# Issuing every second regrouping copy of a talking-heads attention from GpSimd

## The chip, the cores and the metric

One core of one Trainium2 chip runs the whole program. The metric is the device time of one execution in microseconds (us). The kernel before took 912.95, 916.15 and 916.83 us in three runs, so its median is 916.15 us.

## What is computed

Three layers follow each other on 1792 tokens (4 batches of 448): an attention whose 12 heads are mixed before and after the softmax ("talking heads"), a feed-forward layer, and a soft mixture of experts.

```python
scores = scale * np.matmul(q, k.transpose(0, 1, 3, 2))
scores = np.einsum('bhij,hg->bgij', scores, w_pre)
scores = scores - np.max(scores, axis=-1, keepdims=True)
attn = np.exp(scores)
attn = attn / (np.sum(attn, axis=-1, keepdims=True) + 1e-09)
attn = np.einsum('bhij,hg->bgij', attn, w_post)
attn_out = np.matmul(attn, v)
...
h = x @ w_in
x = (h - np.tanh(h)) @ w_out
...
logits = x @ phi        # softmaxes over tokens and over slots, 8 experts of 4 slots each
```

All tensors are float32. The change lies in the first layer alone.

## The kernel before

**Chunks and steps.** Each batch's 448 rows are cut into chunks of 120, 120, 120 and 88 rows, 16 chunks in all. TensorE makes the scores of a chunk head by head (`scores`), and ScalarE copies them into the tile `S`, which has the chunk's rows on partitions and heads by keys along them. The mix over heads needs the heads on partitions. So a chunk is taken in 12 (for the short chunk 10) steps of up to 10 rows, and for each step one DMA, the regrouping copy (`regroup`, line 312), moves the 10 rows with their 12 heads from `S` into 120 partitions of a tile `D`: 120 pieces of 1792 bytes, 210 KB. There are 184 steps.

**The order in a step.** The loop at line 566 writes out the order of the work by hand. In every step `s` it first issues the regrouping copy of step `s + 4` (`D_AHEAD`), then the loads and stores planned for this step. Steps are worked off in pairs. In an even step TensorE runs `premix(s)` on the two tiles `D` of steps `s` and `s + 1` (line 321), VectorE takes the maxima (325), TensorE runs `postmix` of the pair four steps back (364), ScalarE the exponentials (333), and GpSimd adds a small number to their sums (`guard`, 339). In the odd step VectorE takes the reciprocal (343), GpSimd multiplies the mixing weights by it (`norm`, two instructions of line 350), and ScalarE gathers the result of `postmix` (378). Scores of the next chunk, value products (403) and conversions of the feed-forward weights (lines 48 to 69) are spread over the steps. Of each of the 64 conversion pieces GpSimd does one addition (line 69).

**Buffers and queues.** There are six tiles `D`, used in turn. So the copy of step `s + 4` needs the tile of step `s - 2`, and has to wait until `premix(s - 2)` has read it. The copy of the odd step after it needs the tile of step `s - 1`, which the same `premix` reads. All DMAs of this stage are issued by SyncE (SP), one after another in the order of the program: the regrouping copies, the loads of `q`, `k`, `v` and raw weights (`f`), and the stores of converted weights (`wi`, `wo`) and of attention results (`xd`). GpSimd issues none.

The names in the diff: `D_AHEAD` is 4, `NH` is 12, `ds` is the list of the six tiles `D`, `chunks[n][2]` the rows of chunk `n`, and `rows(s)` gives a step's chunk, first row and number of rows.

Of the kernel before, what the change touches and what calls it, by code (L numbers as in the profile page):

```python
# [16 lines left out]
NB, NH, SEQ, HD = 4, 12, 448, 64  # L17
# [113 lines left out]
def talking_heads(tc, ident, q, k, v, w_pre, w_post, xd, box, follow):  # L131
    nc = tc.nc
# [4 lines left out]
    D_AHEAD = 4  # L137
# [17 lines left out]
    S_t, D_t = {}, {}  # L155
# [147 lines left out]
    def rows(s):  # L303
        n, kk = slots[s]
        o, m = chunks[n][3][kk]
        return n, o, m

    def regroup(s):
        n, o, m = rows(s)
        t = ds[s % DB]  # L310
        ni, w = chunks[n][2], len(chunks[n][3])
        nc.sync.dma_start(out=t[4:4 + m * NH], in_=S_t[n][o:ni:w])
        D_t[s] = t

    def premix(s):
# [133 lines left out]
    for m in range(1, NC):  # L449
        w = len(chunks[m - 1][3])  # L450
# [11 lines left out]
    for m in range(1, NC):  # L462
        if chunks[m][1] + CHUNK >= SEQ and m + 1 < NC:
            w = len(chunks[m - 1][3])
            w0 = start[m - 1] - D_AHEAD
            free_at = {}
            for p in range(NP):
                t = w0 + HEAD_LAG + p // 2 * w // 3 + 1 + p % 2
# [16 lines left out]
    t = 2  # L485
    for i, j in enumerate(pieces):
# [10 lines left out]
        t = h  # L497
# [18 lines left out]
    for hi, lo, cost, f, a in sorted(wanted, key=lambda z: (z[0] - z[1], z[0])):  # L516
        s = min(range(lo, hi + 1), key=crowd)
# [36 lines left out]
    for s in range(D_AHEAD):  # L554
        regroup(s)
# [9 lines left out]
    s = 0  # L565
    while s < NS + T_LAG + 3 or jobs or late:
# [3 lines left out]
        if s + D_AHEAD < NS:  # L570
            regroup(s + D_AHEAD)
# [898 lines left out]
```

## Time and profile before

| what | value |
|---|---|
| median of three runs | 916.15 us (912.95 to 916.83) |
| the profiled execution | 922.78 us, its span 921.1 us |
| TensorE matmul busy | 841.1 us (91% of the span) |
| ScalarE, VectorE busy | 574.2 us (62%), 559.1 us (61%) |
| GpSimd busy | 250.6 us (27%) |
| DMA | 224.53 MB, mean 244 GB/s |

The span is the time from the first to the last instruction of the profiled execution. Busy times leave out instructions that only wait or issue a DMA. In rows of the trace, PE is TensorE's matmuls, PEld its weight loads, DVE is VectorE, ACT ScalarE, POOL GpSimd and SPq the queue of SyncE. `out<-in` names tiles, L312 is line 312. The attention with its steps takes the first 465 us or so of the span.

### The profile page before, as it was taken

What the parts mean: (1) busy time and instruction counts of PE and PEld (TensorE: products, weight loads), DVE (VectorE), ACT (ScalarE), POOL (GpSimd) and SP (SyncE); (2) the same over time, 40 slices, a digit from 0 to 9 for tenths busy, and PEclk for the clock granted to TensorE, in tenths of its full rate; (3) what the DMA queues carried; (4) which work ended last, traced back from release to release, by engine and by line L of the source; (5) the groups of instructions that cost most, each with busy time, mean ns of one, the idle gap of its engine ahead of it and who ended that gap; (6) DMA issues with size and microseconds to landing.
All of it is one profiled execution on the core that took longest, in us unless ns stands there. A gap on an engine that the chain in (4) does not pass through costs nothing.

```text
span 921.1 us, 28684 instructions
## 1 busy us (share of the span) xinstructions
PE 841.1 (91%) x11750; PEld 599.0 (65%) x11750; DVE 559.1 (61%) x1183; ACT 574.2 (62%) x1351; POOL 250.6 (27%) x431
## 2 busy tenths in 40 slices
PE   7868998979998798999979999999999998999995
PEld 6536666656666566766668777667776776875553
DVE  2445776757777577788545567566766677740103
ACT  2756786857877687888756576546664666730013
POOL 3134343534444344455412223000000014610000
PEclk7988998999999999999989999999999999998998
DMA  4699797997988978787467968669764536879998
GB/s 109 180 194 217 232 232 215 231 224 217 234 235 229 228 220 223 220 248 239 152 226 234 320 236 306 222 252 353 304 216 161 171 110 217 301 308 425 424 374 311
DMA packets 147286, 224.53 MB, mean 244 GB/s; under 512 B 61268, under 2 KB 128852, under 8 KB 143572
## 3 DMA queue, kind: packets, MB, share of 16 engines
q1 hardware_dynamic: 143808, 209.84, 73.4%
q10 hardware_dynamic: 3348, 12.87, 3.7%
q8 instruction: 93, 1.52, 0.7%
q14 instruction: 37, 0.30, 0.1%
HBM read 147.96 MB, written 36.18 MB: 200 GB/s over the span
## 4 chain that ended last, share of the span: by engine, by line
PE 64%; DMA 12%; ACT 9%; DVE 8%; issue 4%; POOL 1%; SPq 1%; ACTq 0%; POOLq 0%; DVEq 0%
PE hp L813 24%; DMA D<-S 8%; PE pm L321 6%; PE vx L403 5%; PE tm L364 5%; PE sc L287 4%; ACT e L333 4%; DVE mx L325 3%; PE h L1255 3%; PE gt L884 3%; PE so L1296 2%; PE tz L1275 2%; ACT S L295 2%; DMA rg<-wi 2%; PE lgp L934 2%
## 5 line engine op out<-in xcount | busy, mean ns | idle before, releaser
L333 ACT ACTIVATE e<-pm,mx 128x448 f32<-128x448 f32 x184 | 115.2, 632 | 94.6 <-DVE mx L325 92.4
L364 PEld LDWEIGHTS tm<-wk,e 64*64 64x64 f32 x5888 | 120.3, 139 | 65.8 <-issue 40.5
L325 DVE TENSOR_REDUCE mx<-pm 128x1 f32<-128x448 f32 x184 | 105.9, 616 | 83.8 <-PE pm L321 83.8
L813 PE MATMUL hp<-xa,rg 128*128 128x512 f32 x576 | 152.4, 404 | 0.0
L364 PE MATMUL tm<-wk,e 64*64 64x60 f32 x5888 | 128.7, 225 | 18.8 <-issue 9.5
L321 PE MATMUL pm<-D,wpre 64*64 64x448 f32 (+2 forms) x736 | 116.3, 579 | 25.0 <-DMA D<-S 19.6
L813 PEld LDWEIGHTS hp<-xa,rg 128*128 128x128 f32 x576 | 102.4, 188 | 28.5 <-issue 10.5
L295 ACT ACTIVATE S<-sc 120x448 f32<-120x448 f32 (+1 forms) x186 | 91.4, 552 | 12.6 <-PE sc L287 6.3
L350 POOL TENSOR_SCALAR wk<-wpost,rv 128x60 f32<-128x60 f32 x184 | 89.6, 510 | 16.0 <-DVE rv L343 13.5
L339 POOL TENSOR_SCALAR rv<-ss 128x2 f32<-128x2 f32 x92 | 26.2, 285 | 248.5 <-ACT e L333 214.8
L287 PE MATMUL sc<-khi,qT 64*120 64x448 f32 (+1 forms) x384 | 85.4, 407 | 6.6 <-DVE xs L413 4.4
L403 PE MATMUL vx<-aT,vn 128*64 128x120 f32 (+1 forms) x1536 | 88.1, 269 | 0.8 <-issue 0.8
L775 POOL TENSOR_TENSOR rg<-rg 128x384 fp32r<-128x384 f32 x32 | 32.0, 1013 | 205.5 <-DVE rg L772 191.7
L403 PEld LDWEIGHTS vx<-aT,vn 128*64 128x64 f32 x1536 | 77.8, 141 | 6.9 <-issue 3.4
L844 DVE SCALAR_TENSOR_TENSOR qd<-qd,sq 128x512 f32<-128x512 f32 (+1 forms) x62 | 38.3, 618 | 69.7 <-ACT mk L840 63.2
L833 ACT ACTIVATE sq<-hp 128x512 f32<-128x512 f32 (+1 forms) x62 | 32.8, 530 | 71.8 <-PE hp L813 71.8
L378 ACT ACTIVATE aT<-tm 128x480 f32<-128x480 f32 x144 | 75.9, 593 | 0.1
L813 PE MATMUL hp<-xb,rg 128*128 128x512 f32 x288 | 74.7, 404 | 0.0
L69 POOL TENSOR_TENSOR fa<-fa,f 128x384 f32<-128x384 f32 x64 | 67.3, 1052 | 8.1 <-DVE rv L343 3.6
L321 PEld LDWEIGHTS pm<-D,wpre 64*64 64x64 f32 (+2 forms) x736 | 25.4, 134 | 63.5 <-DMA D<-S 25.1
L813 PEld LDWEIGHTS hp<-xb,rg 128*128 128x128 f32 x288 | 52.0, 188 | 16.6 <-issue 6.3
L287 PEld LDWEIGHTS sc<-khi,qT 64*120 64x120 f32 (+1 forms) x384 | 46.9, 182 | 22.7 <-issue 5.4
(184 smaller groups left out, 1393.5 us busy)
## 6 DMA issues: line engine op xcount, KB each, us to landing
ex<-in_moe_w_dram SPq DMA_DIRECT2D x25, 1536.0 KB
D<-S SPq DMA_DIRECT2D x144, 210.0 KB
rg<-wis SPq DMA_DIRECT2D x32, 768.0 KB
f<-in_moe_w_in_dram SPq DMA_DIRECT2D x32, 384.0 KB
f<-in_moe_w_out_dram SPq DMA_DIRECT2D x32, 384.0 KB
wis<-rg ACTq DMA_DIRECT2D x16, 768.0 KB
rg<-wi SPq DMA_DIRECT2D x26, 384.0 KB
wi<-fa SPq DMA_DIRECT2D x32, 192.0 KB
```

The source lines that it names most:

```text
L69: eng.tensor_tensor(out=out, in0=bits(a), in1=bits(p), op=ALU.add)
L287: nc.tensor.matmul(xs[e][0][:ni], lhsT=qT[n][s, l, p, :ni], rhs=kt[s], start=(i == 0), stop=(i == 2))
L295: nc.scalar.activation(out=dst, in_=xs[e][0][:ni], func=ACTF.Copy)
L321: nc.tensor.matmul(xs[x][64 * i:64 * i + 64], lhsT=wpre[k0:k1], rhs=d[i][k0:k1], start=True, stop=True)
L325: nc.vector.tensor_reduce(out=mx[:, x:x + 1], in_=xs[x], op=ALU.max, axis=AX.X, negate=True)
L333: nc.scalar.activation(out=es[x], in_=xs[x], func=ACTF.Exp, bias=mx[:, x:x + 1], accum_out=ss[:, x:x + 1])
L350: nc.gpsimd.tensor_scalar(out=wk, in0=wpost, scalar1=rv[:, x:x + 1], scalar2=None, op0=ALU.mult)
L364: nc.tensor.matmul(xs[i][64 * z:64 * z + 64, x, c], lhsT=es[x][h, j:j + 64], rhs=wks[x][h], start=True, stop=True)
L378: nc.scalar.activation(out=out[:, :, c0:c0 + m].rearrange("p a (x i) -> p a x i", x=2), in_=x, func=ACTF.Copy)
L403: nc.tensor.matmul(x[64 * e:64 * e + 64, i, :ni], lhsT=nat_v[b, h // NP][:, h % NP, c, :], rhs=a[:, c, h, :ni], start=(c == 0), stop=(c == ...
L813: nc.tensor.matmul(hp, lhsT=r32(w[:, m, hl, cs]), rhs=r32(x_of(b, c, l)), start=(c == 0 and i == 0), stop=(c == KD - 1 and i == 2))
L844: nc.vector.scalar_tensor_tensor(out=qd, in0=qd, scalar=TG_E, in1=sq, op0=ALU.add, op1=ALU.mult)
```

## The change

In `regroup`, the copies of even steps from step 4 on are issued from GpSimd's queue; the first four and all odd ones stay on SyncE's. That is 90 of the 184 copies. What is copied, from where and to where, and the place of the call in the program stay as they are; nothing else is edited.

```diff
@@ -309,7 +309,8 @@
         n, o, m = rows(s)
         t = ds[s % DB]
         ni, w = chunks[n][2], len(chunks[n][3])
-        nc.sync.dma_start(out=t[4:4 + m * NH], in_=S_t[n][o:ni:w])
+        queue = nc.gpsimd if s >= D_AHEAD and s % 2 == 0 else nc.sync
+        queue.dma_start(out=t[4:4 + m * NH], in_=S_t[n][o:ni:w])
         D_t[s] = t
```

## Rows read from the trace of the kernel before

**Rows 1.** The page: the chain that ended last, shares of the span by line.

```profile
PE hp L813 24%; DMA D<-S 8%; PE pm L321 6%; PE vx L403 5%; PE tm L364 5%; PE sc L287 4%; ACT e L333 4%; DVE mx L325 3%; PE h L1255 3%; PE gt L884 3%; PE so L1296 2%; PE tz L1275 2%; ACT S L295 2%; DMA rg<-wi 2%; PE lgp L934 2%
```

**Rows 2.** Stretches: start:end and length, busy us per engine (instructions), clock, DMA share.

```profile
26.00:465.00 439.00, 389.55 (x8502) 276.69 (x8502) 301.21 (x693) 330.19 (x864) 181.79 (x344) 0.96 0.84 221
...
44.00:83.00 39.00, 28.28 (x510) 18.74 (x507) 18.73 (x44) 23.16 (x58) 13.88 (x32) 0.82 0.98 199
...
178.00:205.00 27.00, 21.98 (x435) 15.31 (x431) 15.78 (x36) 16.10 (x41) 10.75 (x19) 0.94 0.94 218
...
270.00:315.00 45.00, 37.33 (x827) 26.20 (x826) 29.92 (x72) 31.49 (x82) 20.25 (x35) 1.00 0.92 234
...
400.00:465.00 65.00, 60.92 (x1580) 44.22 (x1574) 46.08 (x109) 51.61 (x135) 29.87 (x59) 1.00 0.67 206
```

**Rows 3.** Who waited for whom: total us, times, longest; one line's durations, ns.

```profile
PEld pm L321 <- DMA D<-S: 25.1, 19, 3.2
PE pm L321 <- DMA D<-S: 19.6, 20, 4.1
...
L312 SPq DMA_DIRECT2D D<-S x184: 714/816/5522, 26.4 to 460.2; - x184
```

**Rows 4.** The chain in order of time, 25:31 and 44:83: start, us, what.

```profile
26.36 2.84 DMA D<-S
...
44.84 7.56 DMA vn<-in_v_dram
...
52.47 11.67 DMA D<-S
```

**Rows 5.** SyncE's queue in order of time, 178:206: start, us, line, copy.

```profile
179.81 0.81 SPq L312 DMA_DIRECT2D D<-S  x1
...
181.25 0.81 SPq L312 DMA_DIRECT2D D<-S  x1
...
184.86 0.83 SPq L312 DMA_DIRECT2D D<-S  x1
186.11 0.34 SPq L118 DMA_DIRECT2D wo<-fa  x1
188.15 0.57 SPq L390 DMA_DIRECT2D xd<-xs  x1
188.82 2.85 SPq L312 DMA_DIRECT2D D<-S  x2
```

**Rows 6.** TensorE in order of time, 178:206: in brackets idle before, and releaser.

```profile
194.87 0.93 PE L321 MATMUL pm<-D,wpre 64*64 64x448 f32 x2 [0.82 <-DMA D<-S]
198.07 0.60 PE L321 MATMUL pm<-D,wpre 64*64 64x448 f32 x3 [2.27 <-DMA D<-S]
```

**Rows 7.** SyncE's own waits, 26:470: total us, times, longest us.

```profile
SPq L312 <- PE tm L364: 53.1, 63, 3.4
...
SPq L390 <- DMA D<-S: 3.4, 2, 1.8
```

**Rows 8.** GpSimd's groups, 26:465: count, busy us, mean ns, idle before and releasers.

```profile
L350 POOL TENSOR_SCALAR wk<-wpost,rv 128x60 f32<-128x60 f32 x180 | 87.9, 512 | 11.1 <-DVE rv L343 8.6 <-PE sc L287 2.2
...
L69 POOL TENSOR_TENSOR fa<-fa,f 128x384 f32<-128x384 f32 x64 | 67.3, 1052 | 8.1 <-DVE rv L343 3.6 <-DVE f L64 0.4
...
L339 POOL TENSOR_SCALAR rv<-ss 128x2 f32<-128x2 f32 x90 | 25.8, 287 | 244.3 <-ACT e L333 210.6 <-DMA D<-S 15.8 <-DMA f<-in_moe_w_in_dram 5.3
```

**Rows 9.** GpSimd in order of time, 178:206 and 436:441.

```profile
184.49 0.95 POOL L350 TENSOR_SCALAR wk<-wpost,rv 128x60 f32<-128x60 f32 x2
187.97 0.22 POOL L339 TENSOR_SCALAR rv<-ss 128x2 f32<-128x2 f32 x1 [2.53 <-ACT e L333]
...
437.03 1.02 POOL L69 TENSOR_TENSOR fa<-fa,f 128x384 f32<-128x384 f32 x1 [0.37 <-DVE f L64]
439.08 0.22 POOL L339 TENSOR_SCALAR rv<-ss 128x2 f32<-128x2 f32 x1 [1.03 <-ACT e L333]
```

**Rows 10.** TensorE in order of time, 438:444.

```profile
439.36 0.98 PE L321 MATMUL pm<-D,wpre 64*64 64x448 f32 x8
...
443.00 0.98 PE L321 MATMUL pm<-D,wpre 64*64 64x448 f32 x8
```

**Rows 11.** VectorE, one group of the conversions, 26:465: as in rows 8.

```profile
L52 DVE TENSOR_SCALAR fa<-fa 128x384 f32<-128x384 f32 x64 | 29.9, 468 | 0.0
```

## The prediction, written before the changed kernel ran

> **What bounds the kernel now.** I read the chain first. TensorE's work leads it, but the regrouping copy D<-S is its second entry with 8% of the span, about 74 us [rows 1]. A copy stands on the chain from its issue to its landing, so those 74 us are not idle time. What TensorE itself stood still for a copy is in the waits: 19.6 us in 20 waits of matmuls, and 25.1 us in 19 waits of weight loads [rows 3]. Weight loads and matmuls overlap, so the two are the same stalls seen twice and not a sum. 25 us (2.7%) is the most that can be won by copies that land earlier.
>
> Next, where the stalls lie. Over the 439 us of the attention the 16 DMA engines are busy to 0.84 and TensorE for 389.55 us [rows 2]. Three stretches stand out, with DMA shares of 0.98, 0.94 and 0.92, in which TensorE idles for 39.00 - 28.28 = 10.7, 27.00 - 21.98 = 5.0 and 45.00 - 37.33 = 7.7 us, together 23 us [rows 2]. That agrees with the 20 to 25 us above. At the end, from 400 to 465 us, the share is 0.67 and TensorE is 94% busy [rows 2].
>
> Then, why a copy is late. With nothing else under way it lands 2.84 us after its issue; in a loaded stretch one takes 11.67 us [rows 4]. Three things lengthen it. The copy queues behind loads on the same DMA engines. SyncE issues one DMA at a time, 0.816 us for a typical copy [rows 3], and first waits for a free tile: 53.1 us in 63 waits [rows 7]. And SyncE waits for the landing of earlier DMAs that have nothing to do with the next one: on the chain a load of v, issued at 44.84, lands 7.56 us later, and only then, at 52.47, the copy goes out [rows 4]; the store of attention results waits twice for copies D<-S, which it neither reads nor writes [rows 7]. So only so many DMAs of SyncE's queue may be under way at once.
>
> **The pair.** `premix` needs both tiles of a pair, and the odd step's copy is issued last: in one stalled pair 181.25 against 179.81, in the next 188.82 against 184.86, with another store or two between [rows 5]. That is 1.4 and 4.0 us later, though both tiles come free with the same `premix`. For the pair whose even copy went out at 184.86, TensorE waits 0.82 us at the first matmul (even tile) and 2.27 us at the third (odd tile; each product is two matmuls in fp32) [rows 6]. The odd copy decides most of the stall.
>
> **The change part by part.** *Removed from SyncE:* 90 issues of 0.816 us [rows 3], 73 us of its queue in 439 us, and the wait for a free tile that stands before each. What was queued behind an even copy, the loads and stores of that step and then the odd copy, moves up. The odd copy gains at least the 0.8 us of the even issue, and at most the whole lag, 1.4 to 4.0 us in the two pairs. I take 0.8 us for every stalled copy, near the lower end, because the DMA engines are nearly full there and an earlier issue partly only queues longer. There are some 20 waits in the trace, in about 15 pairs (an estimate: pairs with two waits count once), so 15 x 0.8 = 12 us. The upper end is all 25 us. The lower end is 0, if the engines' rate alone sets the time.
>
> *Added to GpSimd:* 90 issues. The trace has no DMA issued there. The nearest rows are the same copy issued by SyncE, 0.71 us at the least and 0.816 at the median [rows 3], GpSimd's own pass over 128 partitions at 1.05 us [rows 8], and as an upper end two such passes, 2.1 us. I take 1.05, an engine's own work on as many rows, so 95 us. In the program the issue stands before `guard`, ahead of which GpSimd idles 244.3 us in 90 times, 2.7 us each [rows 8]; it is waiting for the exponentials there. That covers 1.05 us in nearly all steps; the thinnest of the rows shown is 1.03 us [rows 9]. At 2.1 us many would reach over by some 0.5 us. What is queued behind is `guard`, then the reciprocal on VectorE, `norm`, and the additions of the conversions. `postmix` uses `norm`'s result only four steps later, so TensorE sees little: 0 to 3 us in all, taken as 1. Without the cover 90 x 1.05 = 95 us would stand on GpSimd's path. GpSimd's busy time goes from 181.79 [rows 2] to 277 of 439 us; it doesn't become the bound.
>
> *Waits moved to GpSimd:* the copy's waits for a free tile and for the chunk's last scores. GpSimd comes to the even copy only after the pair's `norm`, which lies well behind the `premix` that frees the tile; and ScalarE writes the scores before the exponentials for which `guard` would wait anyway. Both cost nothing.
>
> *Later start of the even copies:* SyncE runs ahead and issues when the tile is free. GpSimd comes to it after its work of the step before. For the copy that SyncE issued at 184.86 it would be ready at 184.49 + 0.95 = 185.44 with `premix` at 194.87, so 9.4 us ahead [rows 6, 9]. Late in the stage it is ready at 437.03 + 1.02 = 438.05 with `premix` at 443.00, 4.95 us ahead [rows 9, 10]. From the even copy's issue 1.05 us go for issuing and at least 2.84 - 0.82 = 2.0 us to land [rows 3, 4], 3.1 in all; the loaded price is up to 11.67. A queue of its own spares it the waiting behind SyncE's loads, so I take 5 us. Then the late pairs are short by 0.1 us and some more where traffic is dense: 2 us in all, between 0 and the 11 us of the third rival.
>
> What comes out: -12 + 1 + 2 = -9 us. On the profiled execution 922.78 becomes 914; it lies 6.6 us over the median of the runs, so for the median 916.15 - 9 = 907 us. The later layers start when the attention ends and are fed by loads issued then; I carry the gain over whole.
>
> Two rules of the Trainium skill bear on this. "DMA: Bandwidth & Descriptors", section "Issuing engines are not separate DMA queues", says that DMAs run on the same 16 engines whoever issues them, and that a second issuer saves only the sequencer's time. By it alone the sum would be nearer 0 than -9. The same page, section "Queues, rings and completion order", says that a copy is spread over the largest number of engines up to 16 that divides the outer dimensions of both sides, for SyncE's queue the lowest-numbered ones; that would be 10 for 120 and 10 rows, and that GpSimd's copies take all 16 or go round. By it the even copies would leave ten crowded engines, and the gain would be larger. No row here shows single engines.
>
> **The rivals.**
> *Same.* The engines' rate is the limit where the stalls are: DMA shares of 0.92 to 0.98 [rows 2] speak for it. What the even copies gain in their own queue is taken from the odd copies and loads, and 15 x 0.8 falls to 15 x 0.2 = 3 us, eaten up by 1 + 2. Time 916, within 4 us. Against it: SyncE waits for landings and free tiles while those shares are reached [rows 7], and the odd copy's lag of 1.4 to 4.0 us is issue order and no lack of rate [rows 5]. The skill's first rule above is this rival.
>
> *Larger gain.* Odd copies move up by the full lag, even ones by the shorter queue: the 20 to 25 us of stalls go nearly whole, some 900 to 895 us. For it: stalls of 0.82 and 2.27 us [rows 6] are no longer than the lags. Against it: those shares again.
>
> *Slower.* One mechanism: the even copies of GpSimd land too late. If issue and landing take 7 us in place of 5, a pair like that at 443.00 is short by 7 - 4.95 = 2 us. Pairs follow each other in 443.00 - 439.36 = 3.64 us there [rows 10], so 400 to 465 us holds about 18. A late `premix` puts off GpSimd's next copies too, and with six tiles the loop closes over three pairs, so about 18 / 3 x 2 = 12 us are lost, with as much again in the dense stretches, against up to 12 us won. Net 0 to +12; at 8 us, +10 and more. It decides from about 6.5 us on. For it: 11.67 us is seen in a loaded stretch [rows 4], and a GpSimd issue is unpriced. Against it: in the last stretch the DMA share is only 0.67 [rows 2]. Place: `premix` waits at its first matmul, on the even tile. Time 916 to 930.
> The skill's page "SBUF — State Buffer", section "SBUF: two separate sides", feeds this rival: descriptors written by GpSimd are held up while VectorE runs an instruction that takes the port pair they share. Here line 52 could be one, 64 times 0.468 us [rows 11], too little to decide by itself.
>
> That the change doesn't do what it says can be left out: the diff changes the issuing queue and nothing else.
>
> **How the numbers follow.** The forecast, 4.6 us to about 15 us faster, has 0.44; the larger gain 0.10; same 0.27; slower by over 4.6 us 0.19. 0.5% of 916 is 4.6 us, about what a measurement of this kernel can tell from no change. Faster is 0.54, same 0.27, slower 0.19. For the range I leave out a gain over 21 us (0.06) and a loss over 6 us (0.14): 895 to 922 us. The forecast's own range is 901 to 911.5.
>
> **What would show it.** Right: 94 copies of line 312 on SyncE, 90 on GpSimd; the odd copy issued about when the even one was; TensorE's waits for D<-S down from 19.6 to about 8 us; the three stretches shorter; GpSimd's idle before line 339 down by about 95 us with no longer period of pairs. Wrong: an issue on GpSimd well over 2 us; waits at the first matmul of `premix` from 400 us on; the same stalls at the third matmul. A changed clock or a longer MoE stage would be nothing that I foresaw.

## The result: the changed kernel is about 1% slower

| | median | runs from .. to | ratio to before, 95% interval |
|---|---|---|---|
| before | 916.49 us | 912.95 .. 918.65 | |
| changed | 929.46 us | 926.93 .. 929.77 | 1.0109 [1.0075, 1.0142] |

The forecast was 907 us with a range of 895 to 922; the kernel was 13 us slower in place of 9 us faster. The changed kernel was timed again beside a later set of experiments (`after2`): 1.0093 [1.0058, 1.0129]. The profiled execution took 926.93 us, with a span of 925.2 us.

Line numbers behind the edit are higher by one: `premix` is now line 322, the copy 313, `guard` 340. The page of the changed kernel has, in its chain by line, the copies' share unchanged at 8% (as in [rows 1]):

```profile
PE hp L814 24%; DMA D<-S 8%; PE vx L404 6%; PE pm L322 6%; PE tm L365 4%; ACT e L334 4%; PE sc L287 4%; DVE mx L326 3%; DMA ex<-in_moe_w_dram 3%; PE gt L885 3%; PE lgp L935 2%; PE so L1297 1%; PE sp L1017 1%; PE h L1256 1%; DMA rg<-wi 1%
```

Its stretches, with the columns of [rows 2], and behind them the last one as it was before:

```profile
26.00:465.00 439.00, 375.23 (x8443) 271.56 (x8446) 299.97 (x688) 326.11 (x854) 235.42 (x433) 0.95 0.91 219
...
44.00:83.00 39.00, 26.87 (x514) 18.68 (x518) 18.84 (x44) 23.11 (x59) 19.06 (x40) 0.82 1.04 197
83.00:178.00 95.00, 82.16 (x1927) 59.94 (x1921) 73.43 (x166) 74.87 (x198) 53.58 (x94) 1.00 0.96 230
```

```profile
83.00:178.00 95.00, 87.61 (x1932) 63.14 (x1934) 71.04 (x163) 74.49 (x197) 39.97 (x73) 0.96 0.86 229
```

In the same 439 us TensorE is busy for 375.23 us; before it was 389.55. In the first dense stretch it idles 39.00 - 26.87 = 12.1 us (before 10.7), and from 83 to 178 us, where the prediction had looked for nothing, 95.00 - 82.16 = 12.8 us (before 95.00 - 87.61 = 7.4). The DMA engines' share rises from 0.84 to 0.91 at 219 GB/s instead of 221: they are busier and move no more.

The clock granted to TensorE is the same over the whole span (0.965; before 0.964), but not in the attention. The trace of the kernel before started slowly (0.80 in its first 26 us, 1.00 in the changed kernel's); from 26 to 465 us it has 0.96 and the changed kernel 0.95. In the timed runs of `after2` the median is 0.964, of the kernel before beside them 0.971. From the first to the last `premix` TensorE stands at the lower of its two clock levels, 1.2 GHz in place of 2.4, for 34.1 us before and 23.9 us in `control` (the kernel before, run once more), and for 44.4 and 39.4 us in the two traces of the changed kernel. All ten falls of the clock in the changed kernel's first trace begin during a wait for a copy or a gap put down to "issue" (explained below), or up to 2 us behind one. At the lower level TensorE starts 12 to 15 matmuls per us, at the upper one 20. The longer time at the lower level is therefore worth another 1 to 8 us, an estimate from these figures. If the stalls bring the falls, which no run varied, a stall costs more than its own length.

TensorE's waits in the changed kernel (who waited for whom: total us, times, longest), beside [rows 3]:

```profile
PE pm L322 <- DMA D<-S: 27.2, 15, 6.0
PE tm L365 <- issue: 11.0, 9, 2.8
...
PE sc L287 <- issue: 3.9, 2, 3.6
PE vx L404 <- issue: 3.5, 1, 3.5
```

The wait that should have fallen from 19.6 to about 8 us rose to 27.2. "issue" is idle time for which the trace has no releaser. In the stretch from the first to the last `premix` it holds ten such gaps over 0.3 us, 17.9 us together, and each ends 1.3 to 1.8 us after a packet of the DMA queue that the page calls "instruction" has come in. I read it as TensorE waiting for its own program to be fetched; in the kernel before all 7 such gaps look the same, and in `control` 7 of 8.

How the copies are issued, from the instructions of tile `D` (durations in ns, min/median/max), and the group of GpSimd's `guard` (as [rows 8]):

```profile
L313 SPq DMA_DIRECT2D D<-S x94: 755/830/4741, 22.0 to 461.1; - x94
L313 POOL DMA_DIRECT2D D<-S x90: 650/656/827, 22.7 to 461.6; - x90
...
DMA to landing us min/median/max: 2.7/6.8/11.8
```

```profile
L340 POOL TENSOR_SCALAR rv<-ss 128x2 f32<-128x2 f32 x90 | 25.1, 279 | 184.4 <-ACT e L334 164.6 <-DMA wi<-fa 6.8 <-DMA D<-S 4.8
```

GpSimd's part went as thought: 0.66 us an issue, about 59 us in all, and its idle time before `guard` fell by 244.3 - 184.4 = 60 us. The whole issue time was covered.

One stall shows what went wrong. SyncE, GpSimd and TensorE of the changed kernel in order of time (start, us, line, form; in brackets idle before, and releaser), leading to the `premix` at 255.21:

```profile
244.35 0.76 SPq L313 DMA_DIRECT2D D<-S  x1
```

```profile
244.59 1.03 POOL L69 TENSOR_TENSOR fa<-fa,f 128x384 f32<-128x384 f32 x1
245.59 0.97 POOL L351 TENSOR_SCALAR wk<-wpost,rv 128x60 f32<-128x60 f32 x2
246.50 0.67 POOL L313 DMA_DIRECT2D D<-S  x1
248.47 0.46 POOL L340 TENSOR_SCALAR rv<-ss 128x2 f32<-128x2 f32 x1 [1.30 <-ACT e L334]
```

```profile
253.07 0.53 PE L287 MATMUL sc<-khi,qT 64*120 64x448 f32 x2
255.21 1.42 PE L322 MATMUL pm<-D,wpre 64*64 64x448 f32 x8 [1.61 <-DMA D<-S]
```

The odd copy goes out at 244.35, with no even copy ahead of it: that is what the prediction wanted. But the even copy now stands behind GpSimd's addition and `norm`, goes out at 246.50, 2.15 us after the odd one, and lands 8.57 us after the start of its issue, at 255.07. TensorE waits 1.61 us, at its first matmul, for the even tile. In this pair the order is only turned round.

Landing times here and below are from the start of a copy's issue to the last semaphore event of that DMA in the trace; medians leave the first four pairs out. The lead is from the start of the issue to the pair's `premix`.

| | lead even / odd, us | landing even / odd, us | pairs whose even copy is last, of 88 |
|---|---|---|---|
| before | 10.3 / 8.2 | 6.4 / 6.2 | 0 |
| control | 10.4 / 8.4 | 7.0 / 6.8 | 0 |
| changed | 8.9 / 10.8 | 6.8 / 7.1 | 61 |
| changed, second trace | 8.9 / 10.3 | 7.0 / 7.4 | 56 |

The odd copy won about 2.3 us of lead, the even one lost 1.5, and `premix` needs both.

### The profile page after: what moved, and what is told of

Its sections match the earlier page's. It is cut to its first block, busy times and chain, and to the rows that moved or that the text cites. A ratio compares the mean times of both kernels' runs of the same rounds, so it can differ in the third digit from the quotient of the medians.

```text
span 925.2 us, 28738 instructions
## 1 busy us (share of the span) xinstructions
PE 826.4 (89%) x11750; PEld 594.3 (64%) x11750; DVE 560.4 (61%) x1183; ACT 573.5 (62%) x1351; POOL 305.0 (33%) x521
## 3 DMA queue, kind: packets, MB, share of 16 engines
q1 hardware_dynamic: 132420, 191.00, 68.9%
q0 software_dynamic: 7200, 18.87, 8.0%
## 4 chain that ended last, share of the span: by engine, by line
PE 62%; DMA 14%; ACT 9%; DVE 8%; issue 5%; POOL 2%; SPq 1%; ACTq 0%; POOLq 0%; DVEq 0%
PE hp L814 24%; DMA D<-S 8%; PE vx L404 6%; PE pm L322 6%; PE tm L365 4%; ACT e L334 4%; PE sc L287 4%; DVE mx L326 3%; DMA ex<-in_moe_w_dram 3%; PE gt L885 3%; PE lgp L935 2%; PE so L1297 1%; PE sp L1017 1%; PE h L1256 1%; DMA rg<-wi 1%
## 5 line engine op out<-in xcount | busy, mean ns | idle before, releaser
L365 PEld LDWEIGHTS tm<-wk,e 64*64 64x64 f32 x5888 | 117.7, 142 | 67.8 <-issue 45.2
L365 PE MATMUL tm<-wk,e 64*64 64x60 f32 x5888 | 121.7, 226 | 19.0 <-issue 11.0
L322 PE MATMUL pm<-D,wpre 64*64 64x448 f32 (+1 forms) x736 | 104.4, 591 | 33.9 <-DMA D<-S 27.2
L814 PEld LDWEIGHTS hp<-xa,rg 128*128 128x128 f32 x576 | 102.4, 188 | 28.6 <-issue 10.7
L287 PE MATMUL sc<-khi,qT 64*120 64x448 f32 (+1 forms) x384 | 85.0, 396 | 12.8 <-DVE xs L414 5.7
L351 POOL TENSOR_SCALAR wk<-wpost,rv 128x60 f32<-128x60 f32 x184 | 89.2, 503 | 15.7 <-DVE rv L344 14.1
L322 PEld LDWEIGHTS pm<-D,wpre 64*64 64x64 f32 (+1 forms) x736 | 23.2, 137 | 61.8 <-issue 22.6
```

Of the source, the lines that this page charges most:

```text
L287: nc.tensor.matmul(xs[e][0][:ni], lhsT=qT[n][s, l, p, :ni], rhs=kt[s], start=(i == 0), stop=(i == 2))
L322: nc.tensor.matmul(xs[x][64 * i:64 * i + 64], lhsT=wpre[k0:k1], rhs=d[i][k0:k1], start=True, stop=True)
L351: nc.gpsimd.tensor_scalar(out=wk, in0=wpost, scalar1=rv[:, x:x + 1], scalar2=None, op0=ALU.mult)
L365: nc.tensor.matmul(xs[i][64 * z:64 * z + 64, x, c], lhsT=es[x][h, j:j + 64], rhs=wks[x][h], start=True, stop=True)
L814: nc.tensor.matmul(hp, lhsT=r32(w[:, m, hl, cs]), rhs=r32(x_of(b, c, l)), start=(c == 0 and i == 0), stop=(c == KD - 1 and i == 2))
```

## The experiments

Three theories. **Late**: an even copy issued by GpSimd starts too late, since it stands behind GpSimd's work of the step before. **Ahead**: SyncE, which no longer issues the even copies nor waits for their tiles, sends its other DMAs sooner, so that more is under way and something else lands later. **Own cost**: a copy issued from GpSimd costs more on the DMA engines wherever it stands.

The table has all runs. "D" and "issue" are TensorE's idle time behind the first matmul of the first `premix` and up to the last `premix`, summed over the matmul records by the releaser the trace gives; each is of one trace. KB is the mean under way there, worked out as bytes times the time from the end of an issue to its landing, over the stretch.

| kernel | ratio, 95% interval | D us | issue us | KB |
|---|---|---|---|---|
| before | | 19.4 | 10.7 | 1258 |
| control | 0.999 [0.995, 1.003] | 14.0 | 14.2 | 1339 |
| changed / after2 | 1.011 / 1.009 | 27.1 / 24.9 | 18.7 / 23.7 | 1434 / 1477 |
| odd_pool | 1.048 [1.042, 1.054] | 57.1 | 1.9 | 996 |
| early_even | 1.009 [1.005, 1.014] | 14.9 | 23.9 | 1369 |
| deep_pool | 1.010 [1.002, 1.018] | 17.0 | 25.8 | 1476 |
| after_brake | 1.010 [1.006, 1.013] | 27.3 | 11.1 | 1315 |
| early_brake | 1.002 [0.999, 1.005] | 14.1 | 17.8 | 1332 |
| deep_brake | 1.001 [0.997, 1.005] | 12.1 | 17.8 | 1308 |
| deep_sync | 1.000 [0.996, 1.004] | 10.5 | 16.2 | 1339 |
| loads_first | 1.008 [1.004, 1.012] | 27.9 | 9.2 | 1264 |
| pair_first | 0.994 [0.991, 0.997] | 15.8 | 10.7 | 1362 |
| pair_pool | 1.005 [1.001, 1.010] | 27.1 | 16.7 | 1497 |
| pair_deep | 1.003 [1.000, 1.006] | 7.1 | 7.6 | 1320 |
| tiny_pool | 1.005 [1.002, 1.009] | 25.2 | 6.0 | 1322 |
| stores_pool | 1.004 [0.999, 1.008] | 17.0 | 17.3 | 1357 |
| light_sync | 0.963 [0.958, 0.968] | 5.2 | 6.5 | 785 |
| light_pool | 0.969 [0.964, 0.974] | 11.1 | 7.4 | 876 |

`control` is the kernel before, run once more; it gives the scatter between traces: its span is 912.4 us where that of [rows 2]'s execution was 921.1, and its waits for D 13.9 where [rows 3] have 19.6. So a single trace tells the place of a loss and not its size to a few us. "issue" too moves between the two, from 10.7 to 14.2 us, which is near the 15 us named beforehand as the mark from which such gaps say nothing about the change. The 24 to 26 us of `after2`, `early_even` and `deep_pool` lie well above it.

> The kernel before, once more, unchanged, for a second trace of it. The first trace of before and the trace of after differ in the attention by 6 us and by 4 us over the span, while the timed medians differ by 13 us; the first had a start at a granted clock of 0.80. Both theories expect a ratio of 1.00 here, TensorE's waits for D<-S near 19.6 us, and its gaps of instruction fetch ('issue') near 11 us. If this trace shows 15 to 19 us of 'issue' too, the eight long fetch gaps of after say nothing about the change.

### Which of the two copies goes to GpSimd, and how late it may be

```diff
+        queue = nc.gpsimd if s >= D_AHEAD and s % 2 else nc.sync
+        queue.dma_start(out=t[4:4 + m * NH], in_=S_t[n][o:ni:w])
```

> The odd copies from GpSimd in place of the even ones, so 90 copies again, of the same size and by the same queue; SyncE keeps the even ones. GpSimd comes to an odd copy after guard of the step before, some 2 us later than to an even one after norm. Theory A (the copies of GpSimd start too late and so are the pair's last): the lead shrinks by about 2 us, waits for D<-S rise well over 27 us, slower than before by 2% or more. Theory B (a copy issued by GpSimd takes more of the DMA engines and so slows every other transfer, the start matters little): the same 1.1% slower as after.

Odd copies from GpSimd: 1.048. The copy that was the last of its pair is now later still: its lead falls to 4.6 us, in the trace it is last in every pair, and TensorE's two kinds of waits for copies are

```profile
PEld pm L322 <- DMA D<-S: 83.4, 45, 5.6
PE pm L322 <- DMA D<-S: 57.1, 31, 4.8
```

Being late costs, then, and in this kernel much; this is the strongest dose of it. That the changed kernel moves the even and not the odd copy is why it loses 1% and not 5%.

`early_even` takes most of the lateness away: an even copy that is not the first of its chunk is issued behind `guard`, two steps earlier in the program.

```diff
+    def early(s):
+        return s >= DB and s % 2 == 0 and slots[s][1] > 0
...
-        if s + D_AHEAD < NS:
+        if s + D_AHEAD < NS and not early(s + D_AHEAD):
             regroup(s + D_AHEAD)
...
                 guard(s)
+                if s + DB < NS and early(s + DB):
+                    regroup(s + DB)
```

> As after, but each even copy that is not the first of its chunk stands behind guard two steps earlier, ahead of norm and the conversion's addition on GpSimd; it waits for the same premix. It can start some 2 us earlier. Theory A: waits for D<-S fall to 10 us or less, ratio 0.99 to 1.00. Theory B: no faster than after (1.01), as the transfers are the same and the engines just as crowded; norm is held up by 0.66 us per pair, which costs 0 to 2 us.

1.009: nothing regained. The even copies' lead is 9.9 us, and they are last in 41 of 88 pairs in place of 61. The waits for copies are back at the level of `control` (13.9), but another kind has grown:

```profile
PE tm L368 <- issue: 16.3, 22, 1.9
PE pm L325 <- DMA D<-S: 15.2, 13, 2.5
PE vx L407 <- issue: 6.7, 3, 4.2
```

So lateness alone doesn't explain the loss. `deep_sync` and `deep_pool` do it another way, with 8 tiles `D` and copies two steps earlier, on SyncE alone and with the even ones on GpSimd:

```diff
-    DB = 6
+    DB = 8
+    FAR = 2
...
+    def far(s):
+        return s >= D_AHEAD + FAR and slots[s][1] > 1
...
-        if s + D_AHEAD < NS:
-            regroup(s + D_AHEAD)
+        for x in (s + D_AHEAD, s + D_AHEAD + FAR):
+            if x < NS and (x - s == D_AHEAD + far(x) * FAR):
+                regroup(x)
```

> All copies on SyncE as before, but eight tiles D in place of six, and each copy that is not one of the first two of its chunk is issued two steps earlier in the program. A baseline for the next run, and a look at what the waits for D<-S are worth when nobody issues from GpSimd: waits down from 14 to 20 us to 5 us or less; 0.5 to 1.5% faster than before if they are what holds the stage up, the same if instruction fetch and the DMA engines take over.

> The same with the even copies on GpSimd, as in after: eight tiles, two steps earlier. The lead of GpSimd's copies grows by one pair, some 4 us, so none should be late. Theory A (the late start alone costs the 13 us): ratio like that of the same kernel with all copies on SyncE, waits for D<-S 5 us or less. Theory B (crowded DMA engines, which also hold up TensorE's instruction fetch): 0.5 to 1% slower than that kernel with D waits just as small, and 18 to 25 us of TensorE's gaps put down to 'issue', against 10 to 15 there.

1.000 and 1.010. In `deep_pool` the leads are 12.7 and 13.1 us and the waits for copies (17.0 us) near those of `control`, and the even copies on GpSimd still cost 1%, again in "issue" (25.8 us). On SyncE the longer lead brings nothing: `deep_sync` still waits 10.5 us for copies, not the 5 us expected. What depth alone is worth these runs don't show, since all four kernels with 8 tiles ran at a lower granted clock, 0.958 to 0.961 in the median of the timed runs, where the kernel before beside them had 0.970 to 0.972. Why stays open.

### Is it the copies' own cost?

`tiny_pool` leaves the regrouping on SyncE and adds, in every even step, a copy of 128 x 16 B of a constant issued from GpSimd; `stores_pool` issues the 64 stores of converted weights from GpSimd and nothing else.

```diff
+        if s >= D_AHEAD and s % 2 == 0:
+            nc.gpsimd.dma_start(out=tiny[s // 2 % 8], in_=ident[:, :4])
...
+    tiny = [lt.tile([128, 4], FP32, tag=f"y{i}", name="tiny", bufs=1) for i in range(8)]
```

```diff
-        self.nc.sync.dma_start(out=dst[:, hf * self.CV:(hf + 1) * self.CV], in_=bits(self.t.pop(j)))
+        self.nc.gpsimd.dma_start(out=dst[:, hf * self.CV:(hf + 1) * self.CV], in_=bits(self.t.pop(j)))
```

> All copies stay on SyncE; beside each even one GpSimd issues a copy of 128 x 16 bytes of a constant into a tile that nobody reads, 90 in all, at the same place of its queue. It has GpSimd's issues and its DMA queue without the bytes and without a reader. If the issue on GpSimd (0.66 us each, 59 us in all) or its mere queue costs the time: 0.5 to 1% slower. Theories A and B both expect 1.00.

> All regrouping copies stay on SyncE; the 64 stores of converted weights (192 KB each, 12.6 MB against the 18.9 MB of the 90 copies) go out from GpSimd. Nothing waits for them soon, so no start can be too late; SyncE is rid of 64 issues of about 0.45 us. Theory A: 0 to 1% faster than before. Theory B: transfers through GpSimd's queue crowd the DMA engines here too, two thirds of the extra engine time of after: 0.3 to 0.8% slower.

1.005, barely clear of no difference, and 1.004, unclear. By themselves they leave room for an own cost: 90 DMAs more on GpSimd cost 0.5%, by the interval 0.2 to 0.9%, more than the first two theories had expected. The instructions of the tile `tiny`:

```profile
L314 POOL DMA_DIRECT2D tiny<-ident x90: 600/606/745, 16.2 to 457.4; - x90
...
DMA to landing us min/median/max: 1.9/5.8/9.4
```

2 KB take a median of 5.8 us to land, against 6.8 for 210 KB in the changed kernel: what is waited for is mostly not the copy's own bytes.

`light_sync` is the kernel before without 59 of the 64 loads of raw feed-forward weights (the conversions use the first five again), `light_pool` the changed kernel with the same loads left out.

```diff
+        n, self.n = self.n, self.n + 1
+        if n >= self.bufs:
+            self.t[j] = [self.kept[n % self.bufs]]
+            return
...
```

> The kernel before without 59 of the 64 loads of raw feed-forward weights (22 MB of the 98 MB of the stage): the conversions work on the five tiles loaded first, so the weights are not the real ones. A baseline for the next run. The DMA engines should be busy to 0.65 to 0.72 in the stage instead of 0.84 to 0.86, waits for D<-S under 10 us, 0 to 2% faster than before.

> The kernel after without the same 59 loads. Theories B and C (crowded DMA engines, deeper queues): with the engines no longer full the difference to the same kernel with all copies on SyncE falls to 0.3% or less. If GpSimd itself, its issues or its late starts cost the time whatever else moves: still 0.8% or more slower than that.

The loads themselves are worth 3.7% of the time, more than all stalls for D. Between the two there remain 0.969 / 0.963 = 1.006, with intervals that overlap, so this pair settles nothing. Even with light traffic the even copy was last in 81 of 88 pairs of `light_pool`.

### Giving SyncE its brake back

If SyncE gets ahead because it no longer issues and waits for the even copies, it must help to give it something small to issue in their place, without taking anything from GpSimd. The brake is a copy of 4 x 16 B into rows of the same tile that nobody reads; like the copy that was there, it has to wait for the tile to come free.

```diff
+        if s >= D_AHEAD and s % 2 == 0:
+            nc.sync.dma_start(out=t[124:128, :4], in_=ident[:4, :4])
```

It was put into `deep_pool`, the changed kernel and `early_even`:

> As the kernel with eight tiles and GpSimd's even copies, but at the old place of each even copy SyncE issues a copy of 4 x 16 bytes into four rows of the same tile that no product reads. SyncE's order, its issues and the turn of its completion semaphores are thereby what they were before the change: the loads no longer move up. Theory C (SyncE, rid of 90 issues, sends its loads earlier; more bytes lie in the DMA queues, 1434 KB against 1257 to 1339 KB, and copies and instruction fetches land later): the bytes in flight fall to 1350 KB or less and the ratio to 1.000 to 1.004. Theory B (a copy of GpSimd costs the DMA engines more): 1.01 as without this brake.

> The changed kernel (even copies from GpSimd), and at the old place of each even copy in SyncE's order a copy of 4 x 16 B from a constant into rows 124 to 127 of the same tile, which nobody reads. It gives SyncE back the issue, the wait for the tile to come free and the completion slot that the even copy used to cost it, and takes no work from GpSimd. If the loss comes from SyncE sending its loads earlier: ratio 1.000 to 1.005 and waits for D plus instruction fetch some 10 us below the changed kernel's. If a copy issued from GpSimd costs the loss by itself: ratio 1.010 or more, since nothing of GpSimd's copies is changed.

> early_even (even copies from GpSimd, those that are not first of their chunk behind the guard two steps earlier; ratio 1.009, waits for D 15 us, instruction fetch 24 us) with one addition: at the old place of each even copy SyncE issues a copy of 4 x 16 B into rows 124 to 127 of the same tile. No tile is added. If the changed kernel's loss has two parts, late even copies and SyncE running ahead, this has neither: 0.998 to 1.004, instruction fetch back near 14 us. If a copy issued from GpSimd costs by itself: still 1.007 or more.

| GpSimd's even copies | SyncE without brake | with brake |
|---|---|---|
| late, as in the change | 1.011, 1.009 | 1.010 |
| early, 6 tiles | 1.009 | 1.002 |
| deep, 8 tiles | 1.010 | 1.001 |

The brake takes back 0.7% (give or take 0.5) with early copies and 0.9% (give or take 0.9) with deep ones, as the intervals give it. As the cause of the 1%, own cost falls here: `early_brake` has 90 copies from GpSimd and 90 DMAs more than before, and is 0.2% slower, by its interval at most 0.5%. Of the two other theories each is enough for the 1%: with late copies the brake doesn't help, and early copies don't help without the brake. The two causes have their own places in the trace. `after_brake` keeps the waits for copies and has less "issue"; `early_brake` has few of the former. First `after_brake`, then `early_brake`, waits as above:

```profile
PE pm L324 <- DMA D<-S: 27.5, 24, 3.3
PE tm L367 <- issue: 8.0, 7, 2.1
```

```profile
PE pm L329 <- DMA D<-S: 14.2, 13, 3.3
PE tm L372 <- issue: 13.1, 16, 3.6
```

D and issue together are 46 to 49 us in the changed kernel's two traces, 38 to 43 in the three with one cause, 30 to 32 in the two with neither, 28 in `control` and 30 in the kernel before. So in the traces the two causes add up, while in the ratios, which are good to 0.3 to 0.8%, one and both can't be told apart. Why the times don't add up too stays open. The clock doesn't settle it: TensorE stands at its lower level for 44.4 and 39.4 us with both causes, 37.5 (`after_brake`), 47.8 and 54.6 us with one, and 37.5 us in each of the two with neither.

That SyncE runs ahead can be seen from what it waits for. A store of converted weights (line 118) needs GpSimd's addition (line 69); when SyncE arrives before the data is there, it waits. SyncE's waits from 26 to 470 us: the changed kernel, `early_even`, `early_brake`, `after_brake`. (`control` has no such row.)

```profile
SPq L118 <- POOL fa L69: 26.0, 12, 3.2
```

```profile
SPq L118 <- POOL fa L69: 34.7, 15, 3.7
```

```profile
SPq L118 <- POOL fa L69: 11.3, 7, 3.1
```

```profile
SPq L118 <- POOL fa L69: 7.8, 4, 2.1
```

`deep_pool` shows only 6.0 us in that row, so it is a sign and no measure. What is under way is larger without the brake (1434, 1477, 1369 and 1476 KB against 1315, 1332 and 1308). That more under way delays the fetch of TensorE's program is a guess which not all numbers fit: `early_even` has 1369 KB and 23.9 us of "issue", `pair_first` below 1362 KB and 10.7 us. It was not varied alone, so how SyncE's running ahead costs time is not shown. Nor was it told apart whether the brake works by its issue, by its wait for the tile, or by its place among the DMAs that SyncE may have open.

### Order on SyncE alone

Copies can be made late or early without GpSimd, too. `loads_first` issues a step's planned loads and stores ahead of its regrouping copy; `pair_first` issues both copies of a pair together, ahead of the loads of both steps; all on SyncE.

```diff
-        if s + D_AHEAD < NS:
-            regroup(s + D_AHEAD)
         for f, *a in at.get(("load", s), []):
             f(*a)
+        if s + D_AHEAD < NS:
+            regroup(s + D_AHEAD)
```

```diff
-        if s + D_AHEAD < NS:
-            regroup(s + D_AHEAD)
+        if s % 2 == 0:
+            for x in range(s + D_AHEAD, min(s + D_AHEAD + 2, NS)):
+                regroup(x)
```

> The kernel before, with each step's planned loads and stores issued ahead of that step's regrouping copy; every copy stays on SyncE and GpSimd issues nothing. If loads that go ahead of copies are what costs: 1.005 to 1.015. If the loss belongs to GpSimd's copies: 1.000, within 0.004.

> The kernel before, with both copies of a pair issued by SyncE one behind the other in the even step, ahead of the loads of both steps. The odd copy's lag behind the even one falls from about 2.1 us to the 0.8 us of one issue, and no copy is on GpSimd. If the odd copy's place behind the even step's loads is what the waits for D cost, as the prediction had it: 0.985 to 0.995, with the waits for D some 5 to 10 us shorter. If landing times set the waits and every wait in SyncE's order holds something else back: 1.000, within 0.004; an odd copy that waits for a tile still being read would hold the loads and give up to 1.01.

> The changed kernel once more, on the chip of these runs: 1.008 to 1.014 by all theories, and a second trace of it. If the division into waits for D (27 us) and instruction fetch (19 us) is chance from run to run, these two move and their sum, about 46 us, stays within 4 us.

1.008 and 0.994. Loads ahead of copies cost about what the change cost, here as waits for copies alone (27.9 us, leads 9.6 and 7.4 us); copies ahead of loads gain 0.6%. Where the gain lies the trace doesn't show: the waits for copies, 15.8 us, lie between those of `control` and of the kernel before (14.0 and 19.4) and did not fall by the 5 to 10 us expected. `pair_first` is the fastest full kernel of the study, 913.7 us against 917.9 for before on that chip, and it is the prediction's idea done by order and not by a second queue: the odd copy follows the even one by 9.5 - 8.2 = 1.3 us in lead, where it was 2.1.

The last two are edits of `pair_first`: the queue of the change, and the depth of `deep_sync` for pairs.

```diff
-        nc.sync.dma_start(out=t[4:4 + m * NH], in_=S_t[n][o:ni:w])
+        queue = nc.gpsimd if s >= D_AHEAD and s % 2 == 0 else nc.sync
+        queue.dma_start(out=t[4:4 + m * NH], in_=S_t[n][o:ni:w])
```

```diff
-    DB = 6
+    DB = 8
+    FAR = 2
...
-            for x in range(s + D_AHEAD, min(s + D_AHEAD + 2, NS)):
-                regroup(x)
+            for x in range(s + D_AHEAD, s + D_AHEAD + FAR + 2):
+                if x < NS and x - x % 2 - s == D_AHEAD + far(x - x % 2 + 1) * far(x - x % 2) * FAR:
+                    regroup(x)
```

> pair_first (0.994) with its even copies issued from GpSimd as in the changed kernel; the odd copy goes on SyncE ahead of both steps' loads. If the prediction's own idea held (the odd copy gains the issue ahead of it): 0.985 to 0.992. If the GpSimd copy is the last of its pair and SyncE is free of its waits, as in the changed kernel: 1.004 to 1.012, with the even copy last in two pairs of three.

> pair_first with 8 D tiles instead of 6, and pairs that have neither step among the first two of their chunk issued two steps earlier still; all on SyncE. If an earlier copy alone shortens the waits: 0.988 to 0.993, with waits for D near 10 us. If what pair_first gained is the odd copy's place ahead of the loads and depth adds nothing (as in deep_sync, 1.000): 0.994, within 0.004.

With the same order and even copies from GpSimd (`pair_pool`) the gain turns to 1.005, with the even copy last in 72 of 88 pairs. Moving the issue to GpSimd costs 1.0054 / 0.9942 = 1.1% in this order too (give or take 0.5). `pair_deep` puts pairs two steps further ahead with 8 tiles. It has the shortest waits for copies of all full kernels, 7.1 us, and is not faster (1.003): TensorE's idle time behind VectorE and GpSimd in the stretch is 23.7 and 10.9 us, in `pair_first` 8.7 and 3.7. The trace tells where most of the first comes from. TensorE's scores wait for VectorE, which takes the results of value products into the one tile `xs`, and VectorE waits for the store of that tile's last content:

```profile
PE sc L288 <- DVE xs L417: 23.0, 12, 4.8
DVE xs L417 <- DMA xd<-xs: 25.3, 5, 6.7
```

In the longest of these waits `xs` was written at 174.85, SyncE issued its store at 184.16, it landed at 192.94, and VectorE went on at 192.97. In `pair_first` VectorE waits 2.9 us for such stores, in `control` 0.4. So for VectorE it is a store of SyncE's queue that comes late, and not a load; whether the copies further ahead push it back was not tested. TensorE also stands at its lower clock level for 54.6 us, in `pair_first` for 23.9. The gain that I expected of either reason didn't come.

## Why the prediction was wrong, step by step

**What bounds.** The bound of 20 to 25 us on the gain was sound, and `pair_deep` shows that it was no more than a bound: with 7.1 us of waits left the time didn't fall. The rows of waits were read as if nothing else could grow in their place. "issue" was not looked at; it holds 10.7 us in the kernel before, 14.2 in `control` and 18.7 to 23.7 in the changed kernel.

**The odd copy gains 0.8 us in 15 pairs: the step that failed, in what it left out.** It did gain lead, 2.3 us in the median, nearer to the full lag than to the 0.8 us taken. But the gain was booked for the pair, and the pair waits for the later of two. The even copy lost 1.5 us of lead at the same time and was the last in 61 of 88 pairs. In two of the three stretches that the prediction named the waits are in fact short: at the pairs from 178 to 205 and from 270 to 315 us they are 11.8 us together before and 3.7 in `control`, 2.1 and 0.7 in the changed kernel's two traces. But from 83 to 178 us, where there had been none (0.0 and 0.1 us), there are now 5.9 and 6.8. With both copies on one queue, the odd one right behind the even one (`pair_first`), the time falls by 0.6%, some 5 us, less than half of the 12 us that the forecast had booked.

**Late even copies cost 2 us: mis-sized, and put in the wrong place.** I took 5 us from issue to landing, "a queue of its own spares it the waiting behind SyncE's loads". It did not. In the last stretch, on which I had worked it out, 4.7 us were measured with a lead of 6.4, and though the even copy was last in 17 of 17 pairs there, little was waited for; TensorE's idle time from 400 to 465 us went only from 4.1 to 6.5. But from 83 to 178 us the median was 7.5 us with a lead of 8.9, and from 44 to 83 single copies took 11 us and more, as the one of 11.67 us in [rows 4] had. Of TensorE's waits for copies in the 88 pairs, 11.0 of 22.2 us stand at pairs whose even copy was last in the first trace, 21.5 of 23.4 in the second; before and in `control` there is no such pair. The rest in the first trace is nearly all from 44 to 83 us, where odd copies took up to 15.5 us. The step took the lead from the quietest stretch and the price from no row at all, though one loaded row was at hand.

**GpSimd's issue** was put at 1.05 us and is 0.66; that work it had waited for anyway hides it was right.

**Removed from SyncE: counted only as a gain.** "What was queued behind moves up" was written of the loads too, and their moving up had no price. `early_even` and `deep_pool` lose 0.9 to 1.0% with waits for copies no longer than in the kernel before, and the brake takes that loss away. This second cause stood in none of the rivals.

**The rivals.** The rival "slower" named the right mechanism and the right mark, the first matmul of `premix`; its time, 916 to 930, held the result. Its place (400 us on) was wrong, and it was only one of two causes: copies that were early again (`early_even`) didn't mend the loss. It had been given 0.19. What fed it too, that VectorE holds up GpSimd's copies, hardly shows: from 400 us on they land in 4.7 us, SyncE's in 4.4 (in the second trace 4.7 and 5.3). "Same" was right in that the DMAs share engines; the Trainium skill's page "DMA: Bandwidth & Descriptors", section "Issuing engines are not separate DMA queues", was closer than the forecast: the changed kernel's landing times are alike on both queues (6.8 and 7.1 us). The other rule, on how a copy is spread, would have given a larger gain. (It stands in the page's section "Why a DMA increments its semaphore by 16 and not by 1", not in the one that the prediction names.) The trace shows only the count of semaphore events, 16 for each copy from GpSimd and 11 for a typical one from SyncE. On which engines the bytes ran no run shows, and no gain came of it.

**What would show it.** Of the marks named beforehand these came out: 94 copies on SyncE and 90 on GpSimd; the odd copy issued no later than the even one; 60 us, not 95, of idle time gone before `guard`. The waits went up, and are now mostly at the first matmul: 22.0 and 21.8 us in the two traces, of 27.5 and 25.2 in all; before it was 8.6 of 19.6.

## What to carry to other kernels

Moving one of two transfers that are needed together to another engine's queue helps only if the moved one doesn't become the later; compare both leads (time from the place where the other engine can issue to the use) with landing times of the busiest stretch, not of the quietest. What stays on the old queue also moves, and a wait that holds back loads may be doing useful work. Where issue order is the trouble, reorder within the queue first: one such order gained 0.6% here and another lost 0.8%, while the second queue lost about 1% in either order that it was tried in. And look at the granted clock of the stretch, not of the span: stalls came with a lower one here.

## What the runs showed of the hardware that I had not expected

A DMA issued from GpSimd costs the engine 0.61 us for 2 KB and 0.66 us for 210 KB, less than the 0.83 us of the same copy on SyncE.

The same 210 KB go out in other packets, and keep the DMA engines busy for longer. DMA queues of `control`, then of the changed kernel (packets, MB, share of 16 engines' span):

```profile
q1 hardware_dynamic: 143808, 209.84, 74.4%
```

```profile
q1 hardware_dynamic: 132420, 191.00, 68.9%
q0 software_dynamic: 7200, 18.87, 8.0%
```

The 90 copies are 18.87 MB. On GpSimd they take 8.0% of 925.2 us, 74 us on each of the 16 engines, most of it in 3504 packets of 5376 B (three rows of 1792 B each). SyncE's queue takes 68.9% of 925.2 us, before 74.4% of 912.4, which is 41 us less than in `control`: its packets of 1792 B take 58 us less on each engine, and all its others 17 us more. Yet `early_brake`, with 7.7% in q0, is as fast as before, so this engine time was not what the change cost.
